# Chunked attention feeding a bilinear feed-forward layer: attention units placed later, transposing loads issued one unit later

## Chip, core and metric

The kernel runs on one core of a Trainium2 chip. The metric is device time in microseconds (us) for one execution, lower being better. TensorE (PE) multiplies matrices into PSUM, VectorE (DVE) and ScalarE (ACT) read PSUM and write on-chip memory, GpSimd (POOL) converts types, and SyncE (SP) issues the DMA transfers. Each of these has its own instruction stream, and waits for the others through semaphores.

## What is computed

The reference, cut to what matters:

```python
# q, k, v: (8, 8, 576, 64); chunks of 64 tokens attend within themselves
scores = scale * q_c @ k_c.transpose(...)
attn = softmax(scores)                    # over the 64 keys of the chunk
x = (attn @ v_c) -> (4608 tokens, 512)
out = ((x @ w_a) * (x @ w_b)) @ w_out     # w_a, w_b: 512 x 1536, w_out: 1536 x 512
```

## The kernel before

**Tiling.** The 4608 tokens are cut into 18 units of 256 and 9 blocks of 512. Block K consists of units 2K and 2K+1. Attention is made unit by unit; the feed-forward layer is made block by block. The order of instructions on every engine is the order in which the program writes them, since the whole body stands in a manual schedule (L476). Which PSUM bank an allocation gets depends on the pool: four banks of `psum` (`ps` in the profile), two of `psum_b` (`pb`), two of `psum_c` (`pc`).

**Attention of a unit U** has four steps. `scores(U)` (L214) makes 64 small matmuls into two banks and two exponentials on ACT into `E`. `sums(U)` (L232) makes four matmuls with ones into two banks and two logarithms on ACT into `ln`. `inverse(U)` (L253) is one exponential over both halves of `ln`, in place. `values(U)` (L260) makes 64 small matmuls into two banks and two DVE multiplications by the inverse, which give one half of `xT` of the block. `values_x(U)` (L560) is `values(U)`, and for an odd unit also `combine_x` (L342): four DVE additions and subtractions of 16-bit tiles, `s1` to `s4`. `bank()` takes the attention's banks from the pools in `spread` in turn.

**Loading.** `load` issues DMAs of q, k and v into fp32 staging; `cast` converts them on POOL. For units 0 to 5 PE transposes q and k (`transpose_pe`, L182); from unit 6 on SP issues two transposing DMAs (`transpose_dma`, L201). `bring(U)` (L298) is, in this order: cast q and k of U, load q of U+1, transposing DMAs of U, cast v of U, load k and v of U+1.

**Block 1** (L565 to L595) is made in 24 half steps `half(ft, u)` of eight matmuls over 256 tokens, an ACT copy and a DVE multiplication. Between the half steps stand, by a list of positions, the transposes and attention of units 3 to 5, `scores(6)`, and the four output tiles of block 0 (`out_step`, 12 matmuls each).

**Blocks 2 to 8** (L629 to L654) use a scheme with seven products for every group i = 0 to 5 of 256 weight columns. A product is eight matmuls of 256 columns. One pass of the loop writes:

```python
now.p1()              # product into A; ACT copies A to B
last.add7()           # DVE: c = C + v, then C += u, for the group before
chunk()               # four matmuls of an output tile; every third adds a DVE copy
last.p3()             # B += ..., DVE multiplies
attend(K, i, 0)       # attention step, if one is set here
now.p6(); now.p2()    # B += ..., ACT copy u; A += ..., ACT copy b
last.p4()             # C += ..., DVE multiplies
chunk()
attend(K, i, 1)       # attention step, if one is set here
now.p5(); now.p7()    # B += ..., ACT copy v; C = ...
```

`now` is the group of this pass and `last` the one before. `p4` writes on top of what `add7` leaves in C, so it waits for the second addition. The table `attention` (L597 to L622) says which attention step stands where; `bring` calls stand at i = 0 and i = 3 of each block. The `chunk` calls of block K work on the output of block K-1, and start at group 1 of block 2.

Of the kernel before, what the change touches and what calls it, by code (L numbers as in the profile page):

```python
# [14 lines left out]
def kernel(  # L15
# [25 lines left out]
    NFT = DFF // 128  # L41
    BLK = 512
    UNIT = 256
    NBLK = NTOK // BLK
    NU = NTOK // UNIT
# [28 lines left out]
    spread = [psum, psum_b, psum, psum_c]  # L74
# [96 lines left out]
    def cast(U, names="qkv"):  # L171
        for n in names if U < NU else "":
            raw[n, U] = raw_pool.tile(
                [128, 2, H, D], BF16, name=f"{n}_raw", bufs=4 if n == "v" else 3
            )
            eng = nc.vector if U == 0 and n != "v" else nc.gpsimd
            eng.tensor_copy(out=raw[n, U], in_=staged.pop((n, U)))  # L177
# [4 lines left out]
    def transpose_pe(U, names="qk"):  # L182
        if U not in qkt:
            qkt[U] = qkt_pool.tile([128, 2, 2, NKT, 128], BF16, name="qkt")
        for n in names:
            w = "qk".index(n)
            src = raw.pop((n, U))
            tp = bank().bitcast(BF16).rearrange("c (i m p) -> c i m p", i=2, m=NKT)
            for i in range(2):
                for m in range(NKT):  # L190
                    nc.tensor.transpose(
                        tp[:, i, m, :],
                        src[:, i, 2 * m:2 * m + 2, :].rearrange("p j d -> p (j d)"),
                        identity,
                    )
            dst = qkt[U][:, w].rearrange("c g m (p i) -> c i m g p", i=2)
            for i in range(2):
                cp = nc.vector.tensor_copy if w == 0 or U == 1 else nc.scalar.copy
                cp(out=dst[:, i], in_=tp[:, i].rearrange("c m (g p) -> c m g p", g=2))
# [86 lines left out]
    def slot(s=None, f=None):  # L286

        if s is not None and s >= NU:
            s = None
        if f is not None:  # L290
            sums(f)
            inverse(f)
        if s is not None:
            scores(s)
        if f is not None:
            values(f)

    def bring(U):  # L298

        cast(U, "qk")  # L300
        load(U + 1, "q")
        if U < NU:
            transpose_dma(U)
        cast(U, "v")
        load(U + 1, "kv")
# [170 lines left out]
    with tc.manual_schedule(  # L476
        engines={
            mybir.EngineType.PE,
            mybir.EngineType.SP,
            mybir.EngineType.DVE,  # L480
            mybir.EngineType.Activation,
            mybir.EngineType.Pool,
        }
    ):

        load(0, "qk")
        load(1, "qk")
        load(0, "v")
        load(1, "v")
        for i in range(3):  # L490
            load_ab(i)
        cast(0, "qk")
        transpose_pe(0)
        cast(1, "qk")
        cast(0, "v")
        cast(1, "v")
        cast_ab(0)
        load_ab(3)
        cast_ab(1)
        cast_ab(2)  # L500
        cast_ab(3)
        transpose_pe(1, "q")
        scores(0)
        transpose_pe(1, "k")
        sums(0, halves=None)
        keep_warm(2)
        scores(1)
        inverse(0)
        values(0)
        keep_warm(1)  # L510
        sums(1, halves=True)
        values(1)
        keep_warm(7)
        load(2, "qk")
        load_ab(4)
        load_ab(5)
        load(2, "v")
        load(3)
        cast(2, "qk")
        cast_ab(4)  # L520
        cast_ab(5)
        cast(2, "v")
        cast(3)
        for j in range(6):
            load_wo(j)
        for j in range(6):
            cast_wo(j)
        load(4)
        load(5)
        spread[:] = [psum]  # L530
        combos = [(i, p) for i in range(NWP) for p in range(4)]

        def combo():
            if combos:
                combine_w(*combos.pop(0))

        for ft in range(NFT):
            ab_step(0, ft)
            if 2 <= ft < 10:
                combo()  # L540
            if ft == 6:
                transpose_pe(2)
            if ft == 7:
                slot(2)
            if ft == 9:
                slot(None, 2)

        cast(4)
        cast(5)
        load(6)  # L550
        for U in range(PE_UNITS, 8):
            bring(U)

        outs = []

        def chunk():
            if outs:
                out_part(*outs.pop(0))

        def values_x(U):  # L560
            values(U)
            if U % 2:
                combine_x(U // 2)

        def half(ft, u):  # L565
            ab_step(1, ft, 256 * u, 256 * u + 256)
            if ft % 4:
                combo()

        seq = [lambda ft=ft, u=u: half(ft, u) for u in range(2) for ft in range(NFT)]  # L570
        def spread_over(*pools):
            spread[:] = pools

        spread_over(psum, psum_b)
        for at, f in reversed([
            (1, lambda: transpose_pe(3)),
            (4, lambda: slot(3)),
            (7, lambda: slot(None, 3)),
            (16, lambda: out_step(0, 0, 1, psum_b)),
            (16, lambda: transpose_pe(4)),  # L580
            (18, lambda: slot(4)),
            (20, lambda: out_step(0, 1, 1, psum_b)),
            (20, lambda: transpose_pe(5)),
            (21, lambda: slot(5, 4)),
            (22, lambda: out_step(0, 2, 1, psum_b)),
            (22, lambda: spread_over(psum, psum_c)),
            (23, lambda: slot(6, 5)),
            (24, lambda: combine_x(2)),
            (24, lambda: out_step(0, 3, 1, psum_b)),
            (24, lambda: spread_over(psum)),  # L590
        ]):
            seq.insert(at, f)
        for step in seq:
            step()
        assert not combos  # L595

        attention = {  # L597
            (2, 0, 0): [lambda: sums(6), lambda: inverse(6)],
            (2, 0, 1): [lambda: values_x(6)],
            (2, 1, 0): [lambda: scores(7)],  # L600
            (2, 1, 1): [lambda: sums(7)],
            (2, 2, 0): [lambda: inverse(7)],
            (2, 2, 1): [lambda: scores(8)],
            (2, 3, 1): [lambda: values_x(7)],
            (2, 4, 0): [lambda: scores(9)],
            (2, 4, 1): [lambda: sums(8)],
            (2, 5, 1): [lambda: inverse(8)],
        }
        for K in range(3, NBLK):
            U = 2 * K + 2  # L610
            for at, f, u in (
                ((0, 0), values_x, U),
                ((0, 1), scores, U + 2),
                ((1, 1), sums, U + 1),
                ((2, 1), inverse, U + 1),
                ((3, 0), values_x, U + 1),
                ((3, 1), scores, U + 3),
                ((4, 1), sums, U + 2),
                ((5, 1), inverse, U + 2),
            ):  # L620
                if u < NU:
                    attention[(K, *at)] = [lambda f=f, u=u: f(u)]  # L622

        def attend(K, i, n):
            for f in attention.get((K, i, n), ()):
                f()

        last = None
        for K in range(2, NBLK):  # L629
            for i in range(NWP):  # L630
                if i == 1:
                    outs += [(K - 1, tg, p) for tg in range(4) for p in range(3)]
                if i in (0, 3):
                    if K == 2 and i == 0:
                        bring(8)
                    if K + 1 < NBLK:
                        bring(2 * K + 5 if i == 0 else 2 * K + 6)
                now = Group(K, i)
                now.p1()
                if last:  # L640
                    last.add7()
                chunk()
                if last:
                    last.p3()
                attend(K, i, 0)
                now.p6()
                now.p2()
                if last:
                    last.p4()
                chunk()  # L650
                attend(K, i, 1)
                now.p5()
                now.p7()
                last = now  # L654
        last.add7()
        chunk()
        last.p3()
        chunk()
        last.p4()
        while outs:  # L660
            chunk()
        for tg in range(4):
            out_step(NBLK - 1, tg, 2 if tg == 3 else 1)
# [30 lines left out]
```

## Time and profile before

| what | value |
|---|---|
| six runs | 321.79 to 324.49 us, median 324.03 us |
| the profiled execution's own time | 321.79 us |
| its span, first to last instruction | 319.7 us |
| granted TensorE clock | 1.000 |
| busy, of the span | PE 94%, weight loads 64%, DVE 65%, ACT 53%, POOL 23% |
| chain that ended last | PE 68%, DMA 9%, DVE 6%, SP's queue 6%, ACT 5% |
| block 1, 42.9 to 84.7 us | PE busy 39.04 of 41.90 us |
| block 2 up to 112 us | PE busy 24.73 of 27.30 us |
| 112 to 300 us | PE busy 187.75 of 188.00 us |

The span lies 2.1 us below the time of the same execution, which is what goes on around the first and last instruction. The busy shares of PE come from start times that are recorded and ends that are modelled: four matmuls of 256 columns that follow each other take 0.435 us from start to start and are shown as 0.60 us long. So a shown idle stretch of PE is some 0.17 us shorter than the time that is lost between two starts.

### The profile page before, as it was taken

What the parts mean: (1) busy time and instruction counts of PE and PEld (TensorE: products, weight loads), DVE (VectorE), ACT (ScalarE), POOL (GpSimd) and SP (SyncE); (2) the same over time, 40 slices, a digit from 0 to 9 for tenths busy, and PEclk for the clock granted to TensorE, in tenths of its full rate; (3) what the DMA queues carried; (4) which work ended last, traced back from release to release, by engine and by line L of the source; (5) the groups of instructions that cost most, each with busy time, mean ns of one, the idle gap of its engine ahead of it and who ended that gap; (6) DMA issues with size and microseconds to landing.
All of it is one profiled execution on the core that took longest, in us unless ns stands there. A gap on an engine that the chain in (4) does not pass through costs nothing.

```text
span 319.7 us, 7925 instructions
## 1 busy us (share of the span) xinstructions
PE 300.9 (94%) x3238; PEld 205.8 (64%) x3238; DVE 206.4 (65%) x346; ACT 169.3 (53%) x307; POOL 74.8 (23%) x76
## 2 busy tenths in 40 slices
PE   2879899997899899999999999999999999999995
PEld 1535477774567576767676767676767677777753
DVE  3346778864446866686668657875777588666551
ACT  1742656255777465655655565556565554544400
POOL 1566665642313322222202120300000000000000
PEclk9999999999999999999999999999999999999999
DMA  7999999999989999999948695941111111122124
GB/s 237 306 377 291 285 365 287 268 223 227 215 212 249 208 205 245 231 194 236 227 107 194 139 220 110 222 99 36 35 33 35 35 33 35 34 50 49 36 66 98
DMA packets 139332, 53.98 MB, mean 169 GB/s; under 512 B 114593, under 2 KB 133281, under 8 KB 139297
## 3 DMA queue, kind: packets, MB, share of 16 engines
q1 hardware_dynamic: 139136, 53.36, 71.1%
q8 instruction: 25, 0.41, 0.5%
q10 hardware_dynamic: 160, 0.13, 0.2%
q14 instruction: 11, 0.08, 0.1%
HBM read 37.75 MB, written 9.44 MB: 148 GB/s over the span
## 4 chain that ended last, share of the span: by engine, by line
PE 68%; DMA 9%; DVE 6%; SPq 6%; ACT 5%; issue 3%; POOL 1%; ACTq 0%; POOLq 0%
PE ps L436 19%; PE pb L373 14%; PE pc L373 10%; PE ps L373 9%; PE ps L327 4%; PE pb L458 3%; DMA st<-in_v_dram 3%; SPq L150 3%; PE ps L458 3%; DMA st<-in_q_dram 3%; DMA st<-in_moe_w_b_dram 2%; ACT ln L247 2%; PE ps L237 1%; SPq L162 1%; PE pc L327 1%
## 5 line engine op out<-in xcount | busy, mean ns | idle before, releaser
L436 PE MATMUL ps<-wo,ab_sb 128*128 128x512 bf16 x336 | 86.2, 379 | 0.0
L373 PEld LDWEIGHTS <-t 128*128 128x128 f16 x672 | 63.0, 98 | 17.2 <-issue 4.9
L411 DVE TENSOR_TENSOR c_sb<-pc,v_sb 128x512 f32<-128x512 f32 x42 | 29.0, 691 | 54.4 <-ACT v_sb L384 54.4
L373 PE MATMUL pb<-s,t 128*128 128x256 f16 x336 | 50.7, 274 | 1.5 <-ACT u_sb L384 1.2
L384 ACT COPY u_sb<-pb 128x512 f32<-128x512 f32 x42 | 24.6, 585 | 50.9 <-PE pb L373 46.1
L373 PE MATMUL ps<-xT,wb 128*128 128x256 f16 x336 | 50.4, 273 | 0.0
L436 PEld LDWEIGHTS <-ab_sb 128*128 128x128 bf16 x336 | 32.9, 98 | 21.7
L373 PEld LDWEIGHTS <-wb 128*128 128x128 f16 x336 | 32.9, 98 | 4.0
L423 DVE TENSOR_TENSOR ab_sb<-pc,c_sb 128x512 bf16<-128x512 f32 x42 | 29.0, 689 | 9.5 <-PE pc L373 9.1
L177 POOL CAST q_raw<-st 128x1024 bf16<-128x1024 f32 x17 | 18.6, 1094 | 64.5 <-DMA st<-in_q_dram 55.3
L384 ACT COPY v_sb<-pb 128x512 f32<-128x512 f32 x42 | 24.7, 587 | 11.8 <-PE pb L373 11.8
L423 DVE TENSOR_TENSOR ab_sb<-pb,b_sb 128x512 bf16<-128x512 f32 x42 | 28.8, 685 | 1.6 <-PE pb L373 1.6
L412 DVE TENSOR_TENSOR pc<-pc,u_sb 128x512 f32<-128x512 f32 x42 | 29.0, 689 | 0.0
L177 POOL CAST k_raw<-st 128x1024 bf16<-128x1024 f32 x17 | 18.0, 1060 | 42.5 <-DMA st<-in_k_dram 42.5
L391 ACT COPY pb<-ps 128x512 f32<-128x512 f32 x42 | 25.0, 594 | 5.5 <-PE ps L373 5.4
L384 ACT COPY b_sb<-ps 128x512 f32<-128x512 f32 x42 | 24.8, 590 | 4.3 <-DVE ab_sb L423 4.3
L279 DVE TENSOR_TENSOR xT<-ps,ln 128x512 f16<-128x512 f32 x31 | 20.0, 683 | 8.8 <-ACT ln L256 8.8
L373 PE MATMUL pc<-xT,t 128*128 128x256 f16 x168 | 25.2, 272 | 0.3 <-DVE pc L412 0.2
L373 PE MATMUL pb<-s,wa 128*128 128x256 f16 x168 | 25.2, 273 | 0.0
L373 PE MATMUL pc<-s,t 128*128 128x256 f16 x168 | 25.2, 273 | 0.0
L230 ACT ACTIVATE E<-ps 128x512 bf16<-128x512 f32 x30 | 16.6, 594 | 13.4 <-PE ps L222 12.6
L373 PEld LDWEIGHTS <-wa 128*128 128x128 f16 x168 | 16.4, 98 | 10.9
(79 smaller groups left out, 373.5 us busy)
## 6 DMA issues: line engine op xcount, KB each, us to landing
out_dram<-o_sb SPq DMA_DIRECT2D x70, 128.0 KB, 2.4
st<-in_v_dram SPq DMA_DIRECT2D x32, 256.0 KB, 4.2
st<-in_q_dram SPq DMA_DIRECT2D x23, 256.0 KB, 4.1
st<-in_k_dram SPq DMA_DIRECT2D x23, 256.0 KB, 3.7
st<-in_moe_w_b_dram SPq DMA_DIRECT2D x6, 512.0 KB, 7.4
st<-in_moe_w_a_dram SPq DMA_DIRECT2D x6, 512.0 KB, 7.8
st<-in_moe_w_out_dram SPq DMA_DIRECT2D x6, 512.0 KB, 6.6
st<-in_q_dram SPq DMA_DIRECT2D x4, 512.0 KB, 5.5
```

The lines of the kernel that those rows point to most:

```text
L177: eng.tensor_copy(out=raw[n, U], in_=staged.pop((n, U)))
L230: nc.scalar.activation(out=E_of[U][:, j], in_=sc[j], func=AF.Exp, scale=scale)
L279: nc.vector.tensor_tensor(out=x_tiles[K][:, :, c0:c0 + 128], in0=av[cl].rearrange("p m g s -> p m (g s)"), in1=rs[:, cl], op=MULT,)
L327: nc.tensor.matmul(ps[n], w_ab[n, i][:, kt, o:o + 128], xT[:, kt, c0:c1], start=(kt == 0), stop=(kt == NKT - 1),)
L373: nc.tensor.matmul(t[:, h * 256:h * 256 + 256], w[:, kt, h * 128:h * 128 + 128], x[:, kt], start=start and h == 0 and kt == 0, stop=h == 1 ...
L384: nc.scalar.copy(out=t, in_=src)
L391: nc.scalar.copy(out=self.B, in_=self.A)
L411: nc.vector.tensor_tensor(out=self.c, in0=self.C, in1=self.v, op=ADD)
L412: nc.vector.tensor_tensor(out=self.C, in0=self.C, in1=self.u, op=ADD)
L423: nc.vector.tensor_tensor(out=self.dst[:, :, c0:c0 + 256], in0=t.rearrange("p (h n) -> p h n", h=2), in1=o.rearrange("p (h n) -> p h n", h=2),
L436: nc.tensor.matmul(out_ps[K, tg], ab_tiles[K][:, ft, tg * 128:tg * 128 + 128], w_out[ft], start=(ft == 0), stop=(ft == NFT - 1),)
L458: nc.tensor.matmul(o_ps, ab_tiles[K][:, ft, tg * 128:tg * 128 + 128], w_out[ft][:, cols], start=(ft == 0), stop=(ft == NFT - 1),)
```

## The change

In block 1 the list of positions becomes straight code, and the work between the half steps stands differently: `values(3)` comes two half steps after `sums(3)`, the first output tile and `transpose_pe(4)` one half step later, `transpose_pe(5)` directly behind the second output tile, and `sums`, `inverse`, `scores` and `values` of units 4 and 5 are set apart by single half steps and output tiles. `scores(6)` leaves block 1. In blocks 2 to 7 each block K now makes the whole attention of units 2K+2 and 2K+3, where block K before also made scores and sums of a later unit. All steps keep their content. The `bring` calls move one unit back: bring(8) and bring(9) at groups 0 and 3 of block 2, where bring(8) and bring(9) stood together at group 0 and bring(10) at group 3.

```diff
     def bring(U):
 
+        if U >= NU:
+            return
         cast(U, "qk")
...
-        for at, f in reversed([
-            (1, lambda: transpose_pe(3)),
-            (4, lambda: slot(3)),
-            (7, lambda: slot(None, 3)),
-            (16, lambda: out_step(0, 0, 1, psum_b)),
-            (16, lambda: transpose_pe(4)),
-            (18, lambda: slot(4)),
-            (20, lambda: out_step(0, 1, 1, psum_b)),
-            (20, lambda: transpose_pe(5)),
-            (21, lambda: slot(5, 4)),
-            (22, lambda: out_step(0, 2, 1, psum_b)),
-            (22, lambda: spread_over(psum, psum_c)),
-            (23, lambda: slot(6, 5)),
-            (24, lambda: combine_x(2)),
-            (24, lambda: out_step(0, 3, 1, psum_b)),
-            (24, lambda: spread_over(psum)),
-        ]):
-            seq.insert(at, f)
...
+        halves = [(ft, u) for u in range(2) for ft in range(NFT)]
+
+        def h(n=1):
+            for _ in range(n):
+                half(*halves.pop(0))
+
+        def normalize(U):
+            sums(U)
+            inverse(U)
+
+        spread[:] = [psum, psum_b]
+        h(1)
+        transpose_pe(3)
+        h(3)
+        scores(3)
+        h(3)
+        normalize(3)
+        h(2)
+        values(3)
+        h(8)
+        out_step(0, 0, 1, psum_b)
+        transpose_pe(4)
+        h(2)
+        scores(4)
+        out_step(0, 1, 1, psum_b)
+        transpose_pe(5)
+        h(1)
+        normalize(4)
+        h(1)
+        scores(5)
+        h(1)
+        values(4)
+        h(1)
+        spread[:] = [psum, psum_c]
+        normalize(5)
+        out_step(0, 2, 1, psum_b)
+        h(1)
+        values_x(5)
+        out_step(0, 3, 1, psum_b)
+        spread[:] = [psum]
...
-        attention = {
-            (2, 0, 0): [lambda: sums(6), lambda: inverse(6)],
-            (2, 0, 1): [lambda: values_x(6)],
-            (2, 1, 0): [lambda: scores(7)],
-            (2, 1, 1): [lambda: sums(7)],
-            (2, 2, 0): [lambda: inverse(7)],
-            (2, 2, 1): [lambda: scores(8)],
-            (2, 3, 1): [lambda: values_x(7)],
-            (2, 4, 0): [lambda: scores(9)],
-            (2, 4, 1): [lambda: sums(8)],
-            (2, 5, 1): [lambda: inverse(8)],
-        }
-        for K in range(3, NBLK):
+        attention = {}
+        for K in range(2, NBLK):
             U = 2 * K + 2
             for at, f, u in (
-                ((0, 0), values_x, U),
-                ((0, 1), scores, U + 2),
-                ((1, 1), sums, U + 1),
-                ((2, 1), inverse, U + 1),
-                ((3, 0), values_x, U + 1),
-                ((3, 1), scores, U + 3),
-                ((4, 1), sums, U + 2),
-                ((5, 1), inverse, U + 2),
+                ((0, 0), scores, U),
+                ((1, 0), sums, U),
+                ((1, 1), inverse, U),
+                ((2, 0), values_x, U),
+                ((2, 1), scores, U + 1),
+                ((3, 1), sums, U + 1),
+                ((4, 0), inverse, U + 1),
+                ((4, 1), values_x, U + 1),
...
                 if i in (0, 3):
-                    if K == 2 and i == 0:
-                        bring(8)
-                    if K + 1 < NBLK:
-                        bring(2 * K + 5 if i == 0 else 2 * K + 6)
+                    bring(2 * K + 4 if i == 0 else 2 * K + 5)
```

More of the change, by code (lines that the diff above doesn't have):

```diff
@@ L568, in half @@
                 combo()
[L570 to L574, printed above, removed]
-        for at, f in reversed([
-            (1, lambda: transpose_pe(3)),
-            (4, lambda: slot(3)),
-            (7, lambda: slot(None, 3)),
-            (16, lambda: out_step(0, 0, 1, psum_b)),
-            (16, lambda: transpose_pe(4)),
-            (18, lambda: slot(4)),
-            (20, lambda: out_step(0, 1, 1, psum_b)),
-            (20, lambda: transpose_pe(5)),
-            (21, lambda: slot(5, 4)),
-            (22, lambda: out_step(0, 2, 1, psum_b)),
-            (22, lambda: spread_over(psum, psum_c)),
-            (23, lambda: slot(6, 5)),
-            (24, lambda: combine_x(2)),
-            (24, lambda: out_step(0, 3, 1, psum_b)),
-            (24, lambda: spread_over(psum)),
-        ]):
-            seq.insert(at, f)
@@ L593 @@
-        for step in seq:
-            step()
-        assert not combos
-        attention = {
-            (2, 0, 0): [lambda: sums(6), lambda: inverse(6)],
-            (2, 0, 1): [lambda: values_x(6)],
-            (2, 1, 0): [lambda: scores(7)],
-            (2, 1, 1): [lambda: sums(7)],
-            (2, 2, 0): [lambda: inverse(7)],
-            (2, 2, 1): [lambda: scores(8)],
-            (2, 3, 1): [lambda: values_x(7)],
-            (2, 4, 0): [lambda: scores(9)],
-            (2, 4, 1): [lambda: sums(8)],
-            (2, 5, 1): [lambda: inverse(8)],
-        }
@@ new lines @@
+        h(2)
[16 more added lines that the diff above has]
+        spread[:] = [psum]
+        assert not halves and not combos
+        attention = {}
+        for K in range(2, NBLK):
```

## The prediction

> **What bounds the kernel.** I read the rows of busy time first, then the waits of PE, then the timeline around each wait. PE is busy 94% of the span. Here are three stretches of it (columns: window, length, then busy us of PE, weight loads, DVE, ACT, POOL, with instruction counts, clock, DMA share, GB/s):
>
> ```profile
> 42.80:84.70 41.90, 39.04 (x527) 28.46 (x525) 29.08 (x60) 22.14 (x47) 20.20 (x20) 1.00 1.08 259
> 84.70:112.00 27.30, 24.73 (x331) 16.94 (x330) 17.32 (x29) 17.55 (x32) 8.80 (x8) 1.00 1.08 231
> 112.00:300.00 188.00, 187.75 (x1930) 133.54 (x1929) 130.04 (x211) 107.26 (x192) 22.95 (x22) 1.00 0.55 119
> ```
>
> The reader sees that PE has holes in block 1 and the first 27 us of block 2, and practically none from 112 us on. PE's instructions are the same after the change, so the time moves by PE's waits alone: those removed up to 112 us and those newly made. The waits of PE that the change can touch (total, times, longest):
>
> ```profile
> PE pb L373 <- ACT u_sb L384: 1.2, 1, 1.2
> PE ps L222 <- DMA qkt<-k_raw: 1.1, 1, 1.1
> PE pb L270 <- ACT ln L247: 0.8, 1, 0.8
> PE pb L458 <- ACT E L230: 0.6, 1, 0.6
> PE pc L270 <- ACT ln L247: 0.5, 1, 0.5
> ...
> PE pb L373 <- ACT pb L391: 0.3, 1, 0.3
> PE ps L222 <- ACT qkt L199: 0.2, 1, 0.2
> PE pc L222 <- DVE ab_sb L336: 0.2, 1, 0.2
> PE pc L373 <- DVE pc L412: 0.2, 1, 0.2
> ```
>
> A wait costs some 0.17 us more than shown, because the modelled end of a matmul (0.60 us for four) overlaps the next start (0.435 us apart). I use start to start.
>
> **Block 1: a gain of 1.85 us.** Five waits lie here: scores(5) for the ACT copy of its transposed k (0.25 us in the timeline), values(4) for a bank that the logarithms hold (0.76), an output tile for the bank of E(5) (0.64), scores(6) (0.22) and values(5) (0.48): 2.35 shown, 3.15 us by the starts. After the change I count from the end of transpose_pe(5). A half step is 0.87 us on PE, an output tile 2.59. ACT has two copies of k (until 1.6 us), the copy of the half step (0.37), the two logarithms (1.09), the inverse (1.06), and only then, at 4.1 us, the copy of the next half step. values(4) is reached by PE at 3.5 us. At that moment the four `psum` banks hold that half step, the scores of unit 5 and the two products of a third half step, so values(4) waits for the copy until 4.5: about 1.05 us. The bank behind it and the first sums of unit 5 add 0.15, an earlier bank 0.1: 1.3 us stay. The gain is 3.15 - 1.3 = 1.85 us; ends: 3.15 if banks come free in time, -0.5 if the wait for ACT is one copy longer on both units. I take the counted value. values(3) is moved behind two half steps, but the wait there (0.4 us, for the same ACT copy behind the logarithms and the inverse) ends by the same chain on ACT: nothing. Unit 5's combine has an output tile of 2.59 us in front of it before p6 needs its s2: hidden; without that tile it would cost about 2 us.
>
> **Start of block 2: 0.5 us.** Before, p6 waits 0.32 for ACT's copy of A, and p5 waits 1.16 for the copy u behind two logarithms and an inverse. After, ACT has the two exponentials of unit 6 (1.09) between the copies: p6 starts 1.25 after p1 as before (0.43 lost, scores lie in front), u is ready at 2.87, and p5, reachable at 2.12, starts at 2.92: 0.80. So 1.23 in place of 1.73.
>
> **Transposing loads: 1.43 us.** scores(9) waits 1.08 (1.25 start to start) for its transposing DMA, and the p4 after it 0.18. After, scores of a unit stand five to six groups behind its bring in place of three and a half (a group is some 5.2 us), so this wait goes. What moves with bring is two transposes (1.3 to 2.6 us each on SP's queue), four to six load DMAs, three POOL casts of 1.04 us. SP meets fewer of them before the stores of block 1, later ones before other stores; six o_sb buffers cover a store, and each load is still issued 15.8 us before its cast is needed. I cost the queues at nothing; if a transpose were still late, it would show 1 us as here.
>
> **Steady blocks: the new wait.** Here is what stands against it all. Before, values_x of an odd unit stands at group 3, position 0, with p6, p2, p4, a chunk, p5, p7, p1, a chunk, p3, p6, p2 between it and the p4 that needs the next add7. After, it stands at group 4, position 1: p4 and a chunk are already behind. DVE runs in program order, so the two xT multiplications and four s operations come ahead of add7. Block 2 before has exactly this placement once, for unit 7 (start, length, engine and line, tiles):
>
> ```profile
> 104.37 0.45 PE L270 MATMUL ps<-E,v_raw 64*64 64x64 bf16 x32
> ...
> 104.75 0.61 PE L373 MATMUL pb<-s,t 128*128 128x256 f16 x4
> 105.09 1.28 DVE L279 TENSOR_TENSOR xT<-ps,ln 128x512 f16<-128x512 f32 x2
> ...
> 106.87 1.31 POOL L177 CAST q_raw<-st 128x1024 bf16<-128x1024 f32 x1 [2.46 <-DMA st<-in_q_dram]
> ...
> 107.20 1.26 DVE L353 TENSOR_TENSOR s<-xT 128x512 f16<-128x512 f16 x1
> ...
> 108.72 0.68 DVE L411 TENSOR_TENSOR c_sb<-pc,v_sb 128x512 f32<-128x512 f32 x1
> ...
> 109.32 0.68 DVE L412 TENSOR_TENSOR pc<-pc,u_sb 128x512 f32<-128x512 f32 x1
> ...
> 110.05 0.60 PE L373 MATMUL pc<-xT,t 128*128 128x256 f16 x4
> ```
>
> p5 starts at 104.75, the second addition ends at 110.00, p4 starts at 110.05: 5.30 us. One s operation took 1.26 in place of 0.42 beside a POOL cast; without that, 4.46. PE's own work from p5 to that p4 is p5, p7, p1 at 0.44, a chunk 0.86, p3, p6, p2: 3.49 us (the same distance is 159.06 to 162.55 where nothing waits). Before, the loads' wait of scores(9) covered it; after, nothing does. So p4 waits 4.46 - 3.49 = 0.97 us, in each of blocks 2 to 7: 6 x 0.97 = 5.82 us. Queued behind the waiting p4 is all of PE. At the old place the distance is 6.15 us, and DVE has 1.24 more to do (a multiplication and an o_sb copy): 5.70, no wait, except where a cast hit the combine, at 173.43 and 205.18 (0.35 and 0.23 start to start). These 0.58 go.
>
> **Casts beside the combine: 1.0 us.** The row: the cast at 168.53 lasts 1.04, and the s operation at 168.59 takes 1.26, 0.84 more than undisturbed. [...] I take the row. Loads end in block 6, so four combines (blocks 2 to 5) can meet a cast; three casts of 1.04 in each 15.8 us against a window of 1.54 make about one chance in two each, often in part: 4 x 0.5 x 0.5 = 1.0. Ends: 0, and 4 x 0.84 = 3.4. [...]
>
> Other new places are covered: sums or scores at position 0 leave u ready 1.76 after p6's start where p5 comes at 2.17; the inverse beside the logarithms delays copy v by 0.6, and p3 then follows it by 0.35.
>
> **Sum.** -1.85 - 0.5 - 1.43 - 0.58 = -4.36; +5.82 + 1.0 = +6.82; net +2.46 us. On the profiled execution: 321.79 + 2.46 = 324.25. The median lies 2.2 above that execution, so the forecast is 324.03 + 2.5 = **326.5 us**, slower by 0.8%.
>
> **Rivals.** *PE makes the waits up (not slower).* [...] It would take place in groups 5 and 0 behind the late p4, and decides from 36% repaid (2.46 of 6.82); all repaid gives 324.03 - 4.36 = 319.7. Against it speak two rows: values at 150.80 and 166.56 lie 15.76 apart, as undisturbed ones do, but those around the wait of 0.35,
>
> ```profile
> 166.56 0.45 PE L270 MATMUL ps<-E,v_raw 64*64 64x64 bf16 x32
> 182.66 0.45 PE L270 MATMUL ps<-E,v_raw 64*64 64x64 bf16 x32
> ```
>
> lie 16.10 apart: a lost 0.34 us stays lost. I follow the rows. *Block 1's bank waits all vanish and no cast meets a combine:* -5.66 + 5.82 = +0.2, so 324.2. The list of free banks speaks against the first half. *Every cast hits:* +2.4 more, 328.9; for it speaks that the cast of v lands 11.7 to 13.8 us after the store that holds SP is let go, where the combine lies at about 13.0 to 14.5. *Transposes still late:* one wait of 1 us, 327.5.
>
> **Chances.** Forecast 0.60, waits repaid 0.12, block 1 clean 0.18, every cast 0.07, transposes 0.03. The forecast's own spread, 324.8 to 328.3, comes from the ends for block 1 and the casts. The range 322.8 to 328.8 leaves out the fully repaid case and the worst casts. A measurement here can tell some 0.5% (1.6 us) from no change. Above 325.65: 0.53 of the forecast, both last rivals: 0.63; within: 0.24, mostly block 1 clean; faster 0.13.
>
> **What would show it.** In the profile after: a row of PE pc L373 waiting for DVE pc L412 with about six waits of 0.8 us shown each, one a block, some near 1.6 beside a cast; no wait for qkt from a DMA; one wait of values(4) of about 0.9 in block 1; u_sb below 1. If that row of pc waits is missing or small, the forecast is wrong, and the time falls below 322.

## The result, and the profile after

Before, the median is 324.18 us over 72 runs (321.37 to 327.36); after, it is 324.12 us over 35 runs (322.89 to 325.83). The ratio is 1.001 with a 95% interval of 0.9994 to 1.0026: no change that can be told. The forecast was 326.5. Here and below, ratios and their intervals leave out the runs more than 1.5% above the fastest of their kernel; medians are over all runs. On a chip with both kernels side by side later, after came to 324.11 us beside 324.82, ratio 0.9977 (0.9957 to 0.9997). The profiled execution of after took 324.93 us, span 322.9, while that of before took 321.79, span 319.7: between the two profiles the change costs 3.1 us, between the medians nothing. That difference is what had to be explained. The medians also stand differently among their own runs: before's lies 2.8 us above its fastest run, after's 1.2 us.

The same parts of after as were shown of before, by their own borders (length, then busy us of PE, weight loads, DVE, ACT, POOL, clock, DMA share, GB/s); block 2 now starts at 83.03:

```profile
42.80:83.03 40.23, 39.16 (x495) 28.01 (x494) 32.02 (x59) 21.50 (x46) 19.89 (x19) 1.00 1.09 261
83.03:112.00 28.97, 27.57 (x326) 19.56 (x325) 18.96 (x33) 17.59 (x32) 7.28 (x7) 1.00 1.08 207
112.00:304.00 192.00, 186.58 (x1974) 131.68 (x1972) 130.76 (x210) 108.48 (x195) 23.93 (x23) 1.00 0.56 120
```

The holes have moved. Up to 112 us PE is now idle 2.5 us (1.07 + 1.40) where it was 5.4 (2.86 + 2.57); from there on it is idle 5.4 us where it was 0.25. PE's waits in after, those that begin after 60 us except small ones (total, times, longest):

```profile
PE pc L375 <- DVE pc L414: 6.1, 6, 1.4
...
PE ps L270 <- ACT b_sb L337: 0.5, 1, 0.5
...
PE pb L375 <- ACT u_sb L386: 0.5, 1, 0.5
```

The row of p4 waiting for the second addition of add7 is there as forecast: six waits, one in each of blocks 2 to 7. From start to start they cost 0.83, 1.57, 1.54, 1.47, 0.83 and 0.83 us, 7.07 in all. No row of scores waiting for a transposing DMA is left. Here is the wait in block 3 (start, length, engine, line, tiles):

```profile
139.57 0.61 PE L375 MATMUL pb<-s,t 128*128 128x256 f16 x4
139.76 1.29 DVE L279 TENSOR_TENSOR xT<-ps,ln 128x512 f16<-128x512 f32 x2 [0.62 <-PE ps L270]
...
141.08 0.42 DVE L355 TENSOR_TENSOR s<-xT 128x512 f16<-128x512 f16 x1
...
141.39 1.04 POOL L177 CAST k_raw<-st 128x1024 bf16<-128x1024 f32 x1 [3.56 <-DMA st<-in_k_dram]
141.54 1.16 DVE L355 TENSOR_TENSOR s<-s,xT 128x512 f16<-128x512 f16 x1
...
143.29 0.68 DVE L413 TENSOR_TENSOR c_sb<-pc,v_sb 128x512 f32<-128x512 f32 x1
143.89 0.69 DVE L414 TENSOR_TENSOR pc<-pc,u_sb 128x512 f32<-128x512 f32 x1
...
144.63 0.60 PE L375 MATMUL pc<-xT,t 128*128 128x256 f16 x4 [1.40 <-DVE pc L414]
```

The reader sees the chain that the prediction worked out: p5 at 139.57, then two xT multiplications, four s operations and the two additions, and p4 5.06 us after p5 where PE's own work takes 3.49. One s operation takes 1.16 us in place of 0.42 while POOL casts k beside it: it begins 0.15 after the cast does and ends 0.27 after the cast's end. Without a cast the wait is 0.83 and not 0.97, because xT starts 0.19 after p5 here and started 0.34 after it in the row that the forecast was taken from.

### The profile page after: what moved, and what is told of

Its sections match the earlier page's. It is cut to its first block, busy times and chain, and to the rows that moved or that the text cites. A ratio compares the mean times of both kernels' runs of the same rounds, so it can differ in the third digit from the quotient of the medians.

```text
span 322.9 us, 7931 instructions
## 1 busy us (share of the span) xinstructions
PE 302.1 (94%) x3238; PEld 205.6 (64%) x3238; DVE 211.1 (65%) x346; ACT 169.5 (52%) x307; POOL 73.6 (23%) x76
## 4 chain that ended last, share of the span: by engine, by line
PE 74%; DVE 8%; DMA 7%; SPq 4%; issue 2%; ACT 2%; POOL 1%; DVEq 0%; POOLq 0%; ACTq 0%
PE ps L438 21%; PE pb L375 15%; PE pc L375 11%; PE ps L375 10%; PE ps L329 4%; PE ps L460 3%; DVE s L355 3%; PE pb L460 3%; DMA st<-in_q_dram 3%; DVE xT L279 3%; SPq L150 2%; DMA st<-in_moe_w_b_dram 2%; DMA st<-in_v_dram 2%; PE ps L270 2%; PE pc L329 1%
## 5 line engine op out<-in xcount | busy, mean ns | idle before, releaser
L177 POOL CAST q_raw<-st 128x1024 bf16<-128x1024 f32 x17 | 17.7, 1040 | 79.4 <-DMA st<-in_q_dram 72.1
L247 ACT ACTIVATE ln<-ps 128x512 f32<-128x512 f32 x31 | 17.1, 596 | 14.3 <-PE ps L237 13.5
```

The lines of the kernel that those rows point to most:

```text
L247: nc.scalar.activation(out=ln_of[U][:, cl].rearrange("p m n -> p (m n)"), in_=sm[cl], func=AF.Ln)
```

## Experiments

They follow the two questions: is the new wait worth what the profile says, and what does the usual execution of before lose that its profile does not show. All but the two that only repeat the profile of before were run beside the kernel before on the same chip; its median there is given with it.

### The new wait alone

```diff
-                ((4, 1), values_x, U + 1),
+                ((4, 1), values, U + 1),
+                ((5, 0), combine_of, U + 1),
```

`combine_of(U)` calls `combine_x(U // 2)`: the four s operations go behind add7.

> The kernel after, with combine_x of the odd unit moved alone from group 4, position 1 to group 5, position 0, behind add7. If the late add7 costs what the profile of after shows (six waits of p4, 6.1 us shown, 7.07 us from start to start), the six waits go and the time falls to about 317 us, ratio to before 0.978. If PE makes such waits up again, it stays near 324, ratio 1.00.

Measured: 317.71 us beside 325.21, ratio 0.9783 (0.9733 to 0.9833). All six waits of p4 are gone from its profile, and blocks 3 to 7 take 31.52 us each, where after's take 32.3 to 33.1. In block 2, p4 now follows p5 by PE's own 3.50 us, though a cast meets an s operation there too (1.26 us at 110.25):

```profile
106.47 0.61 PE L375 MATMUL pb<-s,t 128*128 128x256 f16 x4
...
109.97 0.60 PE L375 MATMUL pc<-xT,t 128*128 128x256 f16 x4
```

The median is 6.4 us below after's, by the two ratios some 7 us; the waits that went are 5.5 to 7.07 us in two profiles of after. So they cost about their full length, and PE makes little or none of it up. Apart from them the change gains about 7 us on the median, where the forecast had 4.36. This kernel is faster than before, and by the ratios faster than after, which did not run beside it.

### The kernel before, profiled again, and scores(9) later

> The kernel before, unchanged, for a second profile. The profiled execution of before took 321.79 us, close to the fastest of 72 (321.37), while the median is 324.18; the sum of waits was made on it. Theory A (late transposes): in an execution near the median the waits of scores(8), scores(9) and scores(10) for their transposing DMAs are longer than the 1.1 us of the first profile, by about as much as the execution is slower than 321.8. Theory B (other waits): they stay near 1.1 us, and the further time lies in block 0 and block 1 or in the start, where the change has no part or another one.

Measured: 322.85 us, and the wait of scores(9) is 1.43 us in place of 1.08. That is 0.35 of the 1.06 us between the two executions. Most of the rest, 0.58, lies ahead of block 2, which starts at 85.28 in place of 84.70. This one does not tell the two theories apart.

```diff
-            (2, 4, 0): [lambda: scores(9)],
+            (2, 5, 0): [lambda: scores(9)],
```

> The kernel before, with scores(9) alone moved from group 4 to group 5 of block 2 (5.3 us later), so that its transposing DMA has that much longer. Theory A: the time falls by more than the 1.43 us of the profile, 2 to 3.5 us (ratio 0.989 to 0.994), and the executions spread less. Theory B: 1 to 1.4 us at most (0.996 to 0.997), spread as before.

Measured: 326.19 us beside 325.21, ratio 1.0031 (1.0000 to 1.0061): a miss for both theories. The profile tells part of the reason. scores(8), which stands ahead of the edit, waits 1.72 us for its own transposing DMA in this execution. Behind it p4 in group 4 waits for add7 behind values(7), 0.97 us from start to start, as the forecast had put it for that place, and scores(10) starts at 123.92 after 0.14 us of waiting for its DMA. So one of these waits was hidden under that of scores(9) and comes into view when it goes.

### Block 1's new order alone

The kernel before with the straight code of block 1, `scores(6)` ahead of `values_x(5)`.

> The kernel before with the new order of block 1 alone (scores(6) stays in block 1, ahead of values_x(5)); table and bring calls as before. Theory A: the gain is what the two profiles show between the first half step and block 2, 1.4 us of waits: ratio 0.995 to 0.996. Theory B: block 1 gives the missing 2 to 3 us too: 3.5 to 4.5 us, ratio 0.986 to 0.989.

Measured: 325.89 us beside 325.21, ratio 1.0008 (0.9979 to 1.0037): no gain in the median, a miss for both again. But in its profile block 2 starts at 82.82, 1.9 us sooner than in the first profile of before. What becomes of it stands in the two rows of scores(8) and scores(9):

```profile
99.75 0.45 PE L222 MATMUL ps<-qkt 64*64 64x64 bf16 x32 [2.45 <-DMA qkt<-k_raw]
...
109.46 0.45 PE L222 MATMUL ps<-qkt 64*64 64x64 bf16 x32 [1.28 <-DMA qkt<-k_raw]
```

PE comes sooner and waits longer: scores(9) starts at 109.46, where it started at 108.61 and 109.58 in the two profiles with the old order. This gave theory C for the next runs: in the kernel before it is the transposing DMAs of units 8 to 10 that set the pace, and whatever PE gains ahead of them is lost there. These runs do not show that part, for 19 of the 22 had a lowered clock. The three others took 322.23, 322.56 and 324.15 us, where such runs of before on this chip have a median of 324.27 (see the section on the clock).

### Fewer bytes in front of the transposes

```diff
         for n in names if U < NU else "":
+            if n == "v" and U >= 8:
+                continue
...
-            eng.tensor_copy(out=raw[n, U], in_=staged.pop((n, U)))
+            if n == "k":
+                last_k[0] = raw[n, U]
+            eng.tensor_copy(
+                out=raw[n, U],
+                in_=last_k[0] if n == "v" and U >= 8 else staged.pop((n, U)),
+            )
```

> The kernel before without the loads of v of units 8 to 17; k's converted tile stands in for v there, so attention's result from unit 8 on is another one. This takes 4.5 MB and some 25 issues off the queue on which the transposing DMAs stand, and leaves PE's work as it is. Theory C: scores(8) to scores(10) no longer wait for DMAs, the time falls by 3 to 4.5 us on the median, to about 320 to 321 us (ratio 0.986 to 0.991), and the executions spread less. Theory D: 1.4 us at most (0.996), spread as before.

Measured: 321.32 us beside 324.35, ratio 0.9921 (0.9893 to 0.9948), 3.0 us less by the medians and 2.6 by the ratio: nearer to theory C, at its lower end or just under it. (The profile reads 5.24 MB less with 18 issues fewer, not 4.5 MB and 25.) In it scores(8) and scores(9) start at 99.61 and 107.96 with no wait, and that kernel's runs lie between 320.75 and 323.81. The same edit in after:

> The kernel after without the loads of v of units 8 to 17; k's converted tile stands in for v there, so attention's result from unit 8 on is another one. Theory C: after no longer has a step that waits for these transfers, so the same loads are worth nothing here: ratio to before 0.997 to 1.005, within 1.5 us of after (casts come at other times and can meet the combines more or less often). Theory D: the 3 us that they were worth in the kernel before are found here too, ratio about 0.991.

Measured: 322.59 us beside 323.99, ratio 0.9975 (0.9949 to 1.0002), and 1.5 us under after. That is at the edge of what theory C allowed, and its row of waits gives a likely source:

```profile
PE pc L383 <- DVE pc L422: 4.1, 6, 0.7
```

Six waits again, but none longer than 0.7 us shown: POOL's casts now come at other times, and none meets the s operations for long. From start to start the six take 5.0 us, against 7.07 and 5.5 in the two profiles of after. So in after these loads matter at least in part through the casts; no scores waits for a transpose in either kernel.

### The parts on their own

> The kernel after with the old order of block 1 (without scores(6), which stands in block 2 as in after): new table and bring calls alone. Theory C: the waits for transposing DMAs are gone as in after, the waits of block 1 are back in place (some 1.5 to 2 us, now not covered by a DMA), so the time lies 1.5 to 2 us above after: 325.5 to 326.5 beside 324.1, ratio to before 1.004 to 1.008. Theory D: block 1 alone gave nothing in the kernel before, so it gives nothing here: ratio as after, 1.001.

The old order of block 1 (without scores(6)) under the new table gave 325.09 us beside 324.35, ratio 1.0030 (1.0005 to 1.0056), 1.0 us above after's 324.1. Its waits for transposing DMAs are gone and those of block 1 are back:

```profile
PE pc L375 <- DVE pc L414: 4.4, 6, 1.0
...
PE pb L270 <- ACT ln L247: 0.8, 1, 0.8
PE pb L460 <- ACT E L230: 0.6, 1, 0.6
```

The ratio lies under theory C's range, and its interval holds C's 1.004 as well as D's 1.001, so by itself it decides nothing. Six waits of p4 take 4.4 us here, 6.1 in the first profile of after and 4.5 in the second. Beside that second profile (323.77 us) this execution (325.52) is 1.75 us longer with the same p4 waits, which is about what block 1's waits are worth.

```diff
-                    bring(2 * K + 4 if i == 0 else 2 * K + 5)
+                    if K == 2 and i == 0:
+                        bring(8)
+                    bring(2 * K + 5 if i == 0 else 2 * K + 6)
```

> The kernel after with the bring calls one unit earlier, as before. Theory C: what takes the waits away is that scores stand some 13 to 27 us later, not the order of the loads; the time is that of after within 1.5 us (ratio to before 0.997 to 1.005). If the loads' order carries a gain of its own (fewer transfers in front of the transposes of units 8 and 9, or casts that meet the combines less often), it is slower than after by over 1.5 us.

Measured: 324.55 us beside 324.35, ratio 1.0024 (0.9996 to 1.0052), like after. The later loads carry no gain of their own that these runs could tell; the scores still stand late after their transposes here, and none waits for them.

```diff
-            (2, 2, 1): [lambda: scores(8)],
+            (2, 3, 0): [lambda: scores(8)],
...
-            (2, 4, 0): [lambda: scores(9)],
+            (2, 5, 0): [lambda: scores(9)],
...
-                ((0, 1), scores, U + 2),
+                ((1, 0), scores, U + 2),
...
-                ((3, 1), scores, U + 3),
+                ((4, 0), scores, U + 3),
```

> The kernel before with the scores of every unit from 8 on moved back by one or two places (5.2 us for unit 9, 2.6 to 5.2 us for the others); loads, block 1 and all other steps as before. Theory C: the pace set by the transposing DMAs of units 8 to 10 is gone without a byte less, so the time falls about as with v's loads left out: 2.5 to 3.5 us, ratio 0.989 to 0.993. Theory D (the gain with fewer loads came from something else, such as faster casts or stores): 1 us at most, ratio 0.997 to 1.000, since moving scores(9) alone gave nothing.

Measured: 322.51 us beside 323.99, ratio 0.9973 (0.9950 to 0.9995): the right way, 1.5 us by the medians and 0.9 by the ratio, less than theory C asked. No scores wait for a DMA in its profile. Against that it has the p4 wait of block 2 unveiled (0.97 start to start where before had 0.18) and two waits for a bank (0.8), where before had two waits of p4 (0.58): 1.0 us of new waits, so the freed scores are worth about 1.9 to 2.5 us. Unit 9's DMA landed at 111.12 here, later than in all three profiles of the kernel before unchanged (108.57, 109.53, 110.24), and this execution took 322.56 us.

> The kernel before with the later scores of the run before last and the new order of block 1. Theory C: with the DMAs' pace out of the way the 1.5 to 2 us of waits that the new order of block 1 takes out now reach the end: 1.5 to 2 us below the later scores alone, ratio to before 0.983 to 0.988. If the new order of block 1 is worth nothing by itself, the ratio is that of the later scores alone.

Measured: 322.35 us beside 323.99, ratio 0.994 (0.991 to 0.9969), against 0.9973 for the later scores alone. That misses theory C's 0.983 to 0.988. Block 1 shows in the ratio at about half the forecast size; the medians differ by 0.2 us, and the intervals overlap.

### Does the waiting itself lower the clock

In 64 of 186 runs of the kernel before on these chips the mean granted clock of the core was below 0.9975, and those runs were 2.0 to 2.7 us longer than the others. Some 1.7 to 1.9 us of that is the lost clock itself, counted as the span times one minus the mean clock. Counted so in every run and taken off, the mean differences to the kernel before on the same chip become estimates at equal clock. Each holds to about 0.6 us:

| kernel | runs below 0.9975 | difference at equal clock, us |
|---|---|---|
| block 1 alone | 19 of 22 | -1.2 |
| scores(9) later | 14 of 22 | +0.1 |
| fewer bytes | 0 of 13 | -2.0 |
| later scores | 1 of 22 | -1.1 |
| later scores and block 1 | 6 of 22 | -1.6 |
| after's table, old block 1 | 0 of 22 | +1.6 |
| after, old bring calls | 1 of 14 | +0.8 |
| after, fewer bytes | 1 of 22 | -0.5 |
| after, second series | 0 of 22 | 0.0 |
| the new wait gone | 1 of 6 | -6.9 |

In after's first series it was 1 of 35. At equal clock block 1's new order is worth 1.2 us in the kernel before, 0.5 with later scores, and 1.6 under the new table. So most of its 1.4 us seems to arrive even while scores wait for DMAs, and the lower clock takes it back in the median. Kernels whose profile has scores waiting for a DMA have the low clock often, the others seldom, but later scores with block 1 has it in 6 of 22 without such a wait.

The next three runs set two answers against each other: theory E, that PE's waits bring the lower clock with them, and rival F, that the two have nothing to do with each other.

> The kernel before with the new order of block 1, whose profile has PE idle 2.45 us before scores(8) and 1.28 us before scores(9), with eight spare matmuls (1.73 us) set ahead of scores(8) and four (0.86 us) ahead of scores(9), on a tile of zeros that nothing reads. [...] Rival F (the lower clock has nothing to do with these waits): still more than half of the executions below 0.9975, and the time as without the spare matmuls or up to 2.6 us above: ratio 0.999 to 1.008.

```diff
-            (2, 2, 1): [lambda: scores(8)],
+            (2, 2, 1): [lambda: keep_warm(8), lambda: scores(8)],
...
-            (2, 4, 0): [lambda: scores(9)],
+            (2, 4, 0): [lambda: keep_warm(4), lambda: scores(9)],
```

Measured: 325.05 us beside 324.82, ratio 1.0007 (0.9972 to 1.0042), with 5 of 14 runs below 0.9975. The share is lower than 19 of 22, but that was on another chip, it fell less than theory E asked (6 of 22 at most), and the time did not fall.

> The kernel before with four spare matmuls (0.86 us) ahead of scores(9), where its profile has PE idle 1.08 us. Theory E: executions with a mean clock below 0.9975, about a third before, become fewer than one in seven, the median falls by about 0.5 to 1.2 us (ratio 0.996 to 0.999). Rival F: a third of the executions as before, the time the same or up to 0.9 us above (ratio 1.000 to 1.003).

Only the second of these two edits, in the kernel before: 325.01 us beside 324.82, ratio 1.0031 (0.9999 to 1.0064), 4 of 14 runs below 0.9975 beside 12 of 43. No effect. Its profile shows why four spare matmuls ahead of scores(9) could do little: scores(8) waited as well, for longer.

```profile
101.72 0.45 PE L222 MATMUL ps<-qkt 64*64 64x64 bf16 x32 [1.94 <-DMA qkt<-k_raw]
...
111.59 0.45 PE L222 MATMUL ps<-qkt 64*64 64x64 bf16 x32 [0.58 <-DMA qkt<-k_raw]
```

> The kernel after, unchanged, beside before on the same chip, with the clock of each execution of both. Theory E: after has a clock below 0.9975 in one of ten executions at most, before in about a third; among executions at 0.9975 or above, after is slower than before by 0.7 to 1.5 us, which the forecast's sum of waits says, and the two medians over all are within 0.8 us. Rival F: both kernels have the same share of low clocks, and after lies level with before among the others too.

Measured: 324.11 us beside 324.82. None of 22 runs of after lies below 0.9975, 12 of 43 of before do. Among the others the medians are 324.12 and 323.90: after 0.2 slower, not the 0.7 to 1.5 that was expected. In this profile of after the six p4 waits are shorter than in the first:

```profile
PE pc L375 <- DVE pc L414: 4.5, 6, 1.1
```

### What the profiles of before say together

> The kernel before, unchanged, once more for its profile. Theory C (transposing DMAs set the pace): scores(8), scores(9) and scores(10) of before start when their transposing DMAs land, whatever PE has done until then; an execution is slower by as much as these land later. So if this one is near the median, some 324 to 326 us, scores(9) starts at 111 us or later (108.6 in the first profile) and the sum of PE's waits for transposing DMAs is 3 us or more. Theory D (start and block 0 make the spread): scores(9) starts late only by as much as block 1 does, and the waits stay at 1 to 1.5 us.

Measured: 323.76 us, and scores(9) starts at 110.29 after a wait of 1.14 us. Block 2 had started 1.6 us later than in the first profile, and the DMAs landed 1.7 us later. That is what theory D said and not what theory C said: PE comes late as well when loads are late, and without the DMA this execution would have gained some 1.3 us, hardly more than the first. The three starts:

```profile
108.61 0.45 PE L222 MATMUL ps<-qkt 64*64 64x64 bf16 x32 [1.08 <-DMA qkt<-k_raw]
109.58 0.45 PE L222 MATMUL ps<-qkt 64*64 64x64 bf16 x32 [1.43 <-DMA qkt<-k_raw]
110.29 0.45 PE L222 MATMUL ps<-qkt 64*64 64x64 bf16 x32 [1.14 <-DMA qkt<-k_raw]
```

All executions in which scores(9) waits for its DMA, in us:

| kernel | block 2 starts | waits shown, scores(8) and (9) | scores(9) starts | time of this execution | time minus start |
|---|---|---|---|---|---|
| before, first profile | 84.70 | 0, 1.08 | 108.61 | 321.79 | 213.18 |
| block 1 alone | 82.82 | 2.45, 1.28 | 109.46 | 322.56 | 213.10 |
| before, second | 85.28 | 0, 1.43 | 109.58 | 322.85 | 213.27 |
| before, third | 86.31 | 0, 1.14 | 110.29 | 323.76 | 213.47 |
| before, scores(9) filled | 85.30 | 1.94, 0.58 | 111.59 | 324.89 | 213.30 |
| block 1, both filled | 84.10 | 2.32, 0.22 | 112.13 | 325.09 | 212.96 |

Six executions of four kernels differ by 3.3 us in time and by 0.5 in the last column: nothing is lost behind scores(9). That column alone does not make the landing the cause, for it is about the same, 213.70, with fewer bytes, where scores(9) waits for nothing. What makes scores(9) start late differs: in the second and third profiles mostly a later block 2, in the lower rows a wait of scores(8) that the first profile does not have at all, and the spare matmuls. In after, scores(9) starts at 128.70 and waits for nothing, although its DMA landed at 112.42.

## Why the prediction was wrong

**What bounds the kernel: half right.** PE's waits decide, and in the kernel before it has practically none from 112 us on. But up to there the waits of one execution are no fixed sum: how long scores(8) and scores(9) wait depends on when PE and the transposes come, and differs from one execution to the next.

**The new wait: right, and its size too.** 0.97 forecast for each block, 0.83 found; casts 1.0 forecast, 2.1 in the first profile (three meetings of 0.64 to 0.74, where the row had 0.84) and 0.5 in the second. Sum 6.82 forecast, 7.07 and 5.50 in two profiles. Moving the s operations alone took out some 7 us, which also settles the rival that PE would make the waits up: it repaid nothing that can be told.

**Block 1: too large by 0.4 us as PE's time, and not seen in the median when made alone.** From the first half step to block 2 the profiles have 41.83 us before and 39.89 after; without the 0.5 of scores(6) that is 1.4 us for 1.85 forecast. The wait of values(4) is 0.65 for 1.05. Alone it gave nothing in the median, with a lower clock in 19 of 22 runs, and an estimated 1.2 us at equal clock. The start of block 2 came out better than forecast (1.08 us from start to start for 1.23, before 1.73).

**The step that failed** is the sentence that carried the sum over, "The median lies 2.2 above that execution, so the forecast is 324.03 + 2.5", and with it the size of the term of the transposing loads. The sentence takes the 2.2 us for an offset that after would have too. It has not: after's median lies 0.8 us below its first profiled execution and 0.3 above its second, and 1.2 us above its fastest run, where before's lies 2.8 above its own. From profile to profile the sum was nearly right: 321.79 + 2.46 = 324.25, and after's profiled executions took 324.93 and 323.77; without the new waits the forecast had 321.79 - 4.36 = 317.43, and the profile of that kernel took 317.22.

Two parts of the offset that the change takes out are seen. One is the transposing loads: the term was 1.43 us from one execution, in which scores(8) does not wait. In four other executions scores(8) waits 1.7 to 2.5 us as well, and removing the waits is worth, at equal clock, about 2.0 us (fewer bytes) or 1.1 plus 1.0 of new waits (later scores). The other is **the lower clock**, which before's profile, at 1.000, could not show: about a third of before's runs have it and hardly any of after's. A third of the runs at 2 to 2.7 us is 0.7 to 0.9 us on the mean. That the waits bring it about is likely from the shares, but the filled waits did not show it, and one kernel has it without them, so it stays open.

A part is not found. At equal clock the change without its combine waits gains 6.9 us; 2.0 for the transposes, 1.2 for block 1, 0.65 for the start of block 2 and 0.58 for the old p4 waits make about 4.4. Some 2.5 us stay open, with an uncertainty of about 1 us.

The rival "block 1 clean and no cast" named 324.2, next to the 324.12 measured. That is luck: values(4) still waits 0.65 us, and three casts met the combine in the first profile.

## What to carry to other kernels

When an engine waits for a transfer, the length of that wait in one profile is no price for the median: take several profiles, look at where the engine comes late by itself and where the transfer holds it, and compare the profiled execution's own time and clock with the spread of the runs before a sum is carried from the one to the other. A constant time from the landing to the end only says that nothing is lost behind it. A step that is moved later to give its input time should be looked at on every engine that it runs on: here four short DVE operations in front of an addition that PE needs gave back, block by block, all that the rest of the change had brought. The better version was to move the users of the transfer, and to leave the DVE operations behind the addition: 0.978 of the time.

## What the runs showed of the hardware

The profile of the kernel with later scores and block 1's new order has an idle PE in block 0, before values(2), while it waits for a late v:

```profile
40.22 0.45 PE L270 MATMUL ps<-E,v_raw 64*64 64x64 bf16 x32 [1.75 <-POOL v_raw L177]
```

and right behind it the granted clock (third column from the right) goes down:

```profile
40.00:42.00 2.00, 1.78 (x36) 0.89 (x37) 1.22 (x2) 0.70 (x1) 1.21 (x2) 0.71 1.19 328
42.00:44.00 2.00, 2.00 (x6) 0.76 (x5) 0.07 (x1) 0.59 (x1) 1.04 (x1) 0.50 1.26 339
44.00:46.00 2.00, 2.00 (x11) 0.93 (x10) 0.69 (x1) 0.59 (x1) 0.81 (x1) 0.94 1.00 355
```

The clock lost in these three stretches is 2 x 0.29 + 2 x 0.50 + 2 x 0.06 = 1.7 us; from the start to 40 us, and from 46 us on, it reads 1.00 in this profile. Ahead of the loss PE had been idle for 1.75 us at a stretch. This is one case of a wait with a lower clock behind it, and no run shows that the one brings the other about. In after, waits of up to 1.40 us in blocks 3 to 5 went with a lower clock in 1 of 35 runs, and the second profile of after has a wait of 1.3 us for v with its clock at 1.000.
